# Gated attention and GEGLU on one core: row-tiled attention with turns of eight key tiles, one pool of eight PSUM banks, q, k, v and split weights by way of DRAM, and w_down's sums kept whole in PSUM

## Chip, cores and metric

The kernel runs on one core of a Trainium2 chip. The metric is the device time of one execution in microseconds, the median of several runs; smaller is better. PE is the matrix engine (TensorE), PEld its weight loads, DVE the vector engine, ACT the scalar engine, POOL GpSimd, SP the engine that sends most DMAs.

## What is computed

B = 1, S = 2048 tokens, D = 448, H = 16 heads of 28, F = 1792, all float32.

```python
def _A_ref(x, wqkv, wo):
    qkv = transpose((x @ wqkv).reshape(B, S, 3, H, Dh), 2, 0, 3, 1, 4)
    q, k, v = qkv[0], qkv[1], qkv[2]
    scores = einsum("bhqd,bhkd->bhqk", q, k) * (Dh ** -0.5)
    p = softmax(scores, axis=-1)
    return einsum("bhqk,bhkd->bhqd", p, v) ... .reshape(B, S, D) @ wo

def _B_ref(x, w_gate, w_up, w_down):
    return (gelu(x @ w_gate) * (x @ w_up)) @ w_down

g = sigmoid((x * gate_w).sum(-1, keepdims=True))
return g * _A_ref(x, wqkv, wo) + (1 - g) * _B_ref(x, w_gate, w_up, w_down)
```

## The kernel before

Nearly all matrix products are made in three passes: each float32 operand is split into a high part that TensorE multiplies fast (type fp32r) and a low part (operand minus high part); then high·high, low·high and high·low are summed. The split is a copy and a subtraction, on ACT, DVE or POOL.

The program has these stages. In the names, `hl` holds both parts of something, `u` is x·w_up, `gs` is x·w_gate, `pt` is a 128x512 tile of exponentials, `ps`, `sc`, `pv`, `pg` and `pd` are PSUM tiles (a bank each).

1. **QKV.** 28 tiles of q and k, transposed, 128 rows by 512 tokens (`pqk`, 308 matmuls), are split by ACT and DVE, and both parts are stored to DRAM (`qkd`, 28 stores of 512 KB). Then 16 tiles of V (`pv`, 176 matmuls); V stays in SBUF (`VA`). During the V tiles `X32`, x once more in a layout for row-tiled matmuls, is loaded and split (`split_x32`, L248 and L249). A bound of each head's scores is worked out for the softmax's shift and stored to `shd`; a branch that is not taken handles inputs for which that bound is too wide.
2. **Attention with the first feed-forward products.** A turn is one head and four key tiles (`TURN = 4`), 64 turns in all. TensorE's rows are used as four groups of 32: a matmul of a score (`sc<-Q,K`, contraction 28 rows and 2 shift rows) and one of x·w_up or x·w_gate (`ps<-X,w`, "cross") run beside each other, one in each row group. Four matmuls together are called a round here. After the rounds of a turn comes its values block (`ps<-pt,V`): four column groups, 32 matmuls in the trace. `plan()` simulates the engines with fixed costs and writes down the order of all of it, once, by hand; every instruction keeps that order on its engine. Four PSUM banks hold scores (`psc`), four the sums of cross products and values (`pss`); a cross group that a values block interrupts is added up in SBUF. Weight chunks of 21 cross products are loaded raw by SP in eight pieces (L262, buffer `wraw`) and split by DVE (L273, L275). Finished u and gs tiles go to DRAM (`ud`). ACT takes the exponential straight from the score's bank (L594), or DVE first copies the score to SBUF (L598). At the end of a head POOL's own DMA queue turns the denominators (`dend`, `r`, `rdend`, `rb`), POOL divides (L566) and stores the head's output (`od`).
3. **Transition.** The last gate block's products (`pg`, 168 matmuls) run after the last turn.
4. **Down.** For pairs of the 14 blocks of F (`FC = 2`) and four token blocks (`tb`): `hidden` loads u and gs, ACT applies gelu (L694), POOL multiplies (L695), ACT and DVE split (L696, L697); `down` sums two blocks in PSUM, and DVE adds each such sum into `acc` in SBUF (L714). `load_wo`, `load_o` and `project` bring wo and the attention's output in between.

The order in which DMAs leave SP is the program's. A DMA waits on SP for the one eight before it (they take eight semaphores in turn), and for the tile that it overwrites.

Of the kernel before, what the change touches and what calls it, by code (L numbers as in the profile page):

```python
# [17 lines left out]
P = 128  # L18
# [6 lines left out]
FC = 2  # L25
NB = NF - 1
ORDER = (NF - 1,) + tuple(range(NF - 1))
TURN = 4
LEAD = 8
FIRST = 16  # L30
RUN = 30
STEP, READ, SEEN = 227, 270, 200
EXP, EXP_OUT, COPY, BACK = 480, 620, 690, 100
VALUES, INTO, OUTOF = 857, 90, 200
AHEAD = 8
# [3 lines left out]
VP = H * VC + 8  # L39
# [4 lines left out]

PAIRS = [(b, w) for b in range(3) for w in (b, 4 + b)] + [(4 + b, b) for b in range(3)] + [(3, 3), (3, 7)]


def plan(count, parted=2, loaded=3):  # L50

    turns = [(h, kt) for h in range(H) for kt in range(0, NKT, TURN)]
    items = [[(i, (h, kt, qb)) for i, (h, k0) in enumerate(turns) for kt in range(k0, k0 + TURN)
              if kt // 2 % 2 == r % 2 for qb in (r // 2 * 2, r // 2 * 2 + 1)] for r in range(4)]
    total = count * 21
    ops = []
    now = act = dve = 0
    bank = [0] * 4
    score = [None] * 4
    pos = [0] * 4  # L60
    held = [False] * 4
    mine = [None] * 4
    free = [0] * 4
    shut = [False] * 4
    part = [False] * 4
    since = [0] * 4
    late = []
    left = [4 * TURN] * len(turns)
    seen = [0] * len(turns)
    turn_now = 0  # L70

    def run_act(i, key, src, ready):
        nonlocal act
        begin = max(act, ready)
        act = begin + EXP
        seen[i] = max(seen[i], begin + EXP_OUT + BACK)
        left[i] -= 1
        ops.append(("exp", key, src))
        return begin + EXP_OUT + BACK

    def run_late(until):
        late.sort(key=lambda a: (a[1], a[0]))
        while late and max(act, late[0][0]) <= until:
            ready, i, key = late.pop(0)
            run_act(i, key, None, ready)
# [6 lines left out]
    def end_score(r):  # L92
        i, key, b, _, keep = score[r]
        score[r] = None
        run_late(now + READ - 200)
        direct = max(act, now + READ) + EXP_OUT + BACK
        copied = max(dve, now + SEEN) + COPY + BACK
        if keep > 3 and copied - (200 if i > turn_now else 100) < direct and len(late) < 5:
            bank[b] = run_dve(now + SEEN)
            ops.append(("copy", key, b))  # L100
            late.append((bank[b], i, key))
        else:
            bank[b] = run_act(i, key, b, now + READ)

    def cross_ready(r):
        return (not shut[r] and pos[r] < total and (held[r] or free[r] <= now) and pos[r] // 21 < parted)

    def clear(r, ready):
        if held[r]:
            held[r] = False  # L110
            mine[r][4] = True
            free[r] = run_dve(ready)
            whole = pos[r] % 42 == 0
            ops.append(("clear", r, pos[r] - 1, part[r], whole))
            part[r] = not whole

    def step():
        nonlocal now
        did = []
        for r in range(4):  # L120
            if score[r]:
                i, key, b, n, _ = score[r]
                ops.append(("score", r, key, n, b))
                score[r][3] += 1
                did.append((r, True))
            elif cross_ready(r):
                ops.append(["cross", r, pos[r], not held[r], False])
                mine[r] = ops[-1]
                held[r] = True
                pos[r] += 1  # L130
                did.append((r, False))
        now += STEP
        for r, s in did:
            if s and score[r][3] == 3:
                end_score(r)
            if not s and pos[r] % 42 == 0:
                clear(r, now + SEEN)

    def run(number, n, count, first):
        nonlocal turn_now  # L140
        turn_now = number
        before, after = -(number - 1) % 4, -number % 4
        todo = [count] * 4
        done = k = 0
        n = max(n, first + 3 * count)
        while k < n or any(todo) or any(score):
            while done < 4 * count and k >= first and min(bank) <= now:
                can = [r for r in range(4) if todo[r] and not score[r]
                       and (r != after or todo[r] > 2 or k >= n - 6)]
                if not can or sum(map(bool, score)) >= 3:  # L150
                    break
                r = max(can, key=lambda r: (r == after and k >= n - 6, not cross_ready(r),
                                            not 0 < -pos[r] % 42 <= 2, todo[r], now - since[r]))
                since[r] = now
                b = bank.index(min(bank))
                bank[b] = 1 << 60
                score[r] = [*items[r].pop(0), b, 0, 4 * count - done]
                todo[r] -= 1
                done += 1
            if k >= n - 6 and not shut[after]:  # L160
                shut[after] = True
                clear(after, now + SEEN)
# [3 lines left out]
    def values(i):  # L166
        nonlocal now, parted, loaded
        h, k0 = turns[i]
        r = -i % 4
        while late and late[0][1] <= i:  # L170
            run_late(max(act, late[0][0]))
# [648 lines left out]
```

## Time and profile before

| | us |
|---|---|
| runs shown | 1095.02, 1092.5, 1093.34; median 1093.34 |
| profiled execution, device time | 1094.65 |
| its span | 1092.9 |
| mean clock of TensorE in it | 0.978 of full |
| qk tiles, until the first V tile | 77.8 |
| V tiles | 44.9 |
| attention, from its first matmul | 721.5 (123.36 to 844.89) |
| transition, until the first `pd` matmul | 36.4 |
| down and wo | 207.7 |
| tail | 4.0 |

How to read the rows that follow. In the page, the busy line gives busy time, share of the span and instructions of each engine. A window row gives start:end and length, then busy time and count of PE, PEld, DVE, ACT and POOL, then TensorE's granted clock (1.00 is full), the share of DMA engines in use and the GB/s that they moved. A group row gives line, engine, operation, output<-inputs, size and count, then busy time and mean ns of one, then the idle time of the engine ahead of them and what ended it. A timeline row gives the start, the length, engine and operation of a run of like instructions, and in brackets the idle time ahead and its releaser. A chain row gives a piece of the chain of work that ended last: start, length, what. A DMA row gives the queue, the count, the KB of one and the median us from issue to landing. Matmuls overlap, so that the mean duration of one (0.38 to 0.40 us) is longer than the step from one to the next.

### The profile page before, as it was taken

To read this page: it belongs to the slowest core of one execution; us is meant where nothing else is said; L and a number is where in the kernel's file an instruction comes from. 1 tells how busy PE (TensorE), PEld (TensorE's weight loads), DVE (VectorE), ACT (ScalarE), POOL (GpSimd) and SP (SyncE) were. 2 spreads that over 40 slices of the span, in tenths; PEclk is the share of its full clock that TensorE was granted. 3 is DMA by queue.
4 is the path that set the end of the run, shared out by engine and by line. 5 is a ranking of instruction groups with operands and counts; after the bars stand their busy time and mean duration, and the time that the engine had idled before them with its cause. 6 is when DMAs were issued, how large, how long until landed. Compare 5 with 4: busy or idle time off the path is not lost.

```text
span 1092.9 us, 28107 instructions
## 1 busy us (share of the span) xinstructions
PE 1024.8 (94%) x11191; PEld 741.9 (68%) x11191; DVE 692.5 (63%) x1121; ACT 654.2 (60%) x1255; POOL 271.4 (25%) x352
## 2 busy tenths in 40 slices
PE   9998599999999999999999999999999279889898
PEld 6887476666666666666767676766676267667787
DVE  5542266776666767586666776767765057777654
ACT  5333277777676767776767676767776044444330
POOL 5320100112122021221220212202212244444642
PEclk9999999999999999999999999999999779999999
DMA  8966244453443443534434444344423365665622
GB/s 268 339 231 155 72 128 123 121 165 114 122 149 104 144 135 110 152 109 142 156 95 141 120 144 150 105 139 127 140 82 92 112 223 174 210 185 185 203 91 101
DMA packets 102264, 160.00 MB, mean 146 GB/s; under 512 B 21360, under 2 KB 49776, under 8 KB 102128
## 3 DMA queue, kind: packets, MB, share of 16 engines
q1 hardware_dynamic: 92912, 144.90, 43.0%
q0 software_dynamic: 8384, 12.47, 4.1%
q8 instruction: 90, 1.47, 0.6%
q10 hardware_dynamic: 832, 0.79, 0.2%
q14 instruction: 46, 0.38, 0.1%
HBM read 107.21 MB, written 50.86 MB: 145 GB/s over the span
## 4 chain that ended last, share of the span: by engine, by line
PE 67%; issue 9%; POOL 6%; DMA 5%; DVE 1%; ACT 1%; SPq 0%; POOLq 0%; DVEq 0%; ACTq 0%
PE ps L205 45%; PE sc L205 20%; POOL g L695 4%; PE pd L205 2%; DMA oraw<-od 2%; DMA gs<-ud 1%; DVE hl L697 0%; ACT g L694 0%; POOL ohl L751 0%; SPq L262 0%; DMA u<-ud 0%; DVE ohl L750 0%; DMA draw<-in_wd 0%; DVE WO L737 0%; DMA dend<-o 0%
## 5 line engine op out<-in xcount | busy, mean ns | idle before, releaser
L205 PE MATMUL ps<-X,w 32*128 32x512 f32 x4536 | 480.9, 393 | 0.7 <-ACT gate L431 0.7
L594 ACT ACTIVATE pt<-sc 128x512 f32<-128x512 f32 x660 | 353.3, 608 | 194.8 <-PE sc L205 191.9
L205 PE MATMUL sc<-Q,K 32*128 32x512 f32 x3072 | 434.2, 404 | 9.0 <-DMA Q<-shd 9.0
L205 PEld LDWEIGHTS ps<-X,w 32*128 32x128 f32 x4536 | 387.1, 184 | 29.9 <-issue 10.1
L205 PEld LDWEIGHTS sc<-Q,K 32*128 32x128 f32 x3072 | 306.2, 183 | 76.1 <-issue 52.6
L598 DVE COPY pt<-sc 128x512 f32<-128x512 f32 x364 | 245.3, 689 | 62.9 <-PE sc L205 58.0
L205 PE MATMUL ps<-pt,V 128*32 128x512 f32 x2048 | 233.0, 595 | 0.1
L594 ACT ACTIVATE pt<-pt 128x512 f32<-128x512 f32 x364 | 221.5, 646 | 0.8 <-DVE pt L598 0.8
L205 PE MATMUL pd<-w,hl 128*128 128x448 f32 x672 | 150.2, 380 | 41.1 <-ACT hl L696 37.5
L205 PEld LDWEIGHTS pd<-w,hl 128*128 128x128 f32 x672 | 128.1, 193 | 62.6 <-ACT hl L696 40.2
L205 PEld LDWEIGHTS ps<-pt,V 128*32 128x32 f32 x2048 | 60.0, 109 | 138.0 <-issue 123.6
L635 DVE TENSOR_TENSOR o<-ps,o 128x512 f32<-128x512 f32 x48 | 33.2, 692 | 110.6 <-PE ps L205 110.6
L695 POOL TENSOR_TENSOR g<-g,u 128x512 f32<-128x512 f32 x56 | 73.3, 1314 | 87.7 <-ACT g L694 80.8
L551 POOL DMA_DIRECT2D dend<-o x64 | 31.7, 502 | 232.6 <-DVE o L635 166.6
L696 ACT ACTIVATE hl<-g 128x512 fp32r<-128x512 f32 x56 | 35.4, 632 | 80.1 <-POOL g L695 80.1
L613 DVE COPY u<-ps 128x512 f32<-128x512 f32 x108 | 72.1, 683 | 2.3 <-PE ps L205 1.3
L205 PE MATMUL pqk<-X,WQK 128*128 128x512 f32 x308 | 72.7, 397 | 0.4 <-ACT X L373 0.2
L275 DVE TENSOR_TENSOR w<-wraw,w 128x512 fp32r<-128x512 f32 x112 | 72.2, 684 | 0.0
L561 POOL DMA_DIRECT2D rdend<-r x16 | 8.9, 555 | 243.0 <-DVE r L560 243.0
L205 PEld LDWEIGHTS pqk<-X,WQK 128*128 128x128 f32 x308 | 57.7, 189 | 15.8 <-POOL WQK L383 1.3
L697 DVE TENSOR_TENSOR hl<-g,hl 128x512 fp32r<-128x512 f32 x56 | 43.6, 779 | 36.5 <-ACT hl L696 35.5
L714 DVE SCALAR_TENSOR_TENSOR acc<-pd,gate,acc 128x448 f32<-128x448 f32 x80 | 51.8, 676 | 8.7 <-PE pd L205 8.7
(78 smaller groups left out, 638.5 us busy)
## 6 DMA issues: line engine op xcount, KB each, us to landing
ud<-u SPq DMA_DIRECT2D x108, 256.0 KB
qkd<-hl SPq DMA_DIRECT2D x28, 512.0 KB
K<-qkd SPq DMA_DIRECT2D x128, 112.0 KB
Q<-qkd SPq DMA_DIRECT2D x128, 112.0 KB
u<-ud SPq DMA_DIRECT2D x56, 256.0 KB
gs<-ud SPq DMA_DIRECT2D x52, 256.0 KB
wraw<-in_wu SPq DMA_DIRECT2D x112, 64.0 KB
wraw<-in_wg SPq DMA_DIRECT2D x112, 64.0 KB
```

Source lines behind the costliest of these rows:

```text
L205: return pin(nc.tensor.matmul(o, lhsT, rhs, start=start, stop=stop))
L275: pin(nc.vector.tensor_tensor(w[:, 1, a], raw[:, a], w[:, 0, a].bitcast(F32), OP.subtract))
L551: pin(nc.gpsimd.dma_start(out=dend[h:h + 1, j * 512:(j + 1) * 512], in_=o[j * 32 + DH:j * 32 + DH + 1]))
L561: pin(nc.gpsimd.dma_start(out=rdend[h].rearrange("(p n) -> p n", p=P), in_=r))
L594: pin(nc.scalar.activation(PT[key], PT[key] if b is None else sc[b], AF.Exp, scale=SCALE))
L598: pin(nc.vector.tensor_copy(PT[key], sc[b]))
L613: pin(nc.vector.tensor_copy(u, ps[r]))
L635: pin(nc.vector.tensor_tensor(sums["o"], po, sums["o"], OP.add))
L695: nc.gpsimd.tensor_tensor(g, g, u, OP.mult)
L696: nc.scalar.activation(hl[:, 0], g, AF.Copy)
L697: nc.vector.tensor_tensor(hl[:, 1], g, hl[:, 0].bitcast(F32), OP.subtract)
L714: nc.vector.scalar_tensor_tensor(acc[:, t], p, g1, acc[:, t], OP.mult, OP.add)
```

## The change

- **Turns.** `TURN = 8`: 32 turns, each with a values block of eight key tiles. 36 tiles for exponentials are managed by `plan()`, as are the eight PSUM banks of one pool (`pk`): scores, cross sums and values take the bank that comes free first. Cross groups are shifted by `OFFSET` so that a group's sum stays in one bank; what the shift leaves over of the first block is done at the end and added (`again`).
- **q and k** are stored once as float32 (28 stores of 256 KB) and reloaded in pieces of 28x512 and 28x256, split by POOL; the shift rows go by POOL's queue, except for the first head.
- **V** is stored to DRAM by four DMAs of ACT's queue (5, 5, 3 and 3 tiles, runs of 580 and 348 bytes) and reloaded head by head (`VH`).
- **w_up and w_gate** are split once by POOL (`prepare`), stored split (`wsd`), and each chunk is loaded split, in eight DMAs of 32x2x512 or 32x2x384.
- **X32** is loaded and split by DVE among the qk tiles.
- **Down** runs token block by token block; the 14 blocks' sums stay in four PSUM banks, and DVE gathers once for each token block. Loads are issued four units ahead, and three units are loaded and multiplied ahead of `pg`. DVE multiplies (L726), ACT copies, DVE subtracts. POOL splits wo and the attention's output. The last head is divided after two units of the down stage.

The core of the diff:

```diff
-TURN = 4
-LEAD = 8
+TURN, LEAD, NPT, FIRST = 8, 4, 36, 16
+OFFSET = (0, 21, 9, 30)
...
-    qkd = dram.tile([2, 2 * D, S], F32, name="qkd")
+    qkd = dram.tile([2 * D, S], F32, name="qkd")
+    vd = dram.tile([P, H, NKT, VC], F32, name="vd")
+    wsd = dram.tile([2 * NF, P, 2, 4, P], F32, name="wsd")
...
+    def prepare(b):
+        raw = fw.tile([P, 4, P], F32, name="wraw", bufs=1)
+        by_sp(raw, src[f])
+        hl = fw.tile([P, 2, 4, P], F32R, name="whl", bufs=1)
+        parts(hl[:, 0], hl[:, 1], raw, pool_copy, pool_sub)
+        by_pool(wsd[b], hl.bitcast(F32))
+    def load_chunk(c):
...
-                pin(nc.sync.dma_start(out=raw[group(r), i:i + n], in_=src[f, 32 * j:32 * j + 32, 0:n]))
+                by_sp(w[group(r), :, i:i + n].bitcast(F32), wsd[b, 32 * j:32 * j + 32, :, 0:n])
...
+            if i == base + n - 1:
+                pin(nc.scalar.dma_start(out=vd[:, :, base:base + n], in_=V[:, :, 0:n]))
...
         def turn(i):
...
+            if h + 1 < H:
+                m0 = k0 // TURN * 2
+                if k0 == 0:
+                    for b in range(2):
+                        load_q(h + 1, b)
+                for m in (m0, m0 + 1):
+                    load_k(h + 1, m)
...
+        load_shift(0, by_sp)
+        load_v(0)
...
-            nc.gpsimd.tensor_tensor(g, g, u, OP.mult)
+        pin(nc.vector.tensor_tensor(u, g, u, OP.mult))
...
+    for n in range(1, 3):
+        multiply(n)
+        split_unit(n - 1)
+    PG = [bank(b) for b in early]
...
+    for n, (tb, f) in enumerate(UNITS):
...
+        if n + 4 < len(UNITS):
+            load_unit(n + 4)
+        if n + 3 < len(UNITS):
+            multiply(n + 3)
+        if n + 2 < len(UNITS):
+            split_unit(n + 2)
...
+        if n == 2:
+            divide()
+        if n == 3:
+            load_wo()
+        if n in (5, 10, 18, 32):
+            load_o((5, 10, 18, 32).index(n))
+        if f == 0 and tb:
+            project(tb)
+        down(n)
```

How it moves instructions, at three places. First SP's queue where the attention begins. `Q<-shd` are the shift rows of the first head, `wraw` raw weight pieces; the names in brackets are what a row waits for (DMAHW0 to DMAHW7 are the semaphores of DMAs, taken in turn). Before:

```order
L262 DMA wraw<-in_wu 32x384 [waits DMAHW3_49]
L262 DMA wraw<-in_wu 32x384 [waits DMAHW4_49]
L304 DMA Q_699<-shd 2x1024 [waits DMAHW5_49]
L304 DMA Q_699<-shd 2x1024 [waits DMAHW6_49]
L262 DMA wraw<-in_wu 32x512 [waits DMAHW3_49,DMAHW4_49,DMAHW1_49,DMAHW7_49,DMAHW0_49,DVE_49]
L262 DMA wraw<-in_wu 32x512 [waits DMAHW0_49]
L262 DMA wraw<-in_wu 32x512 [waits DMAHW1_49]
L262 DMA wraw<-in_wu 32x512 [waits DMAHW2_49]
```

And now, where `VH` is the first head's V, `qraw` the second head's raw q:

```order
L218 DMA Q_731<-shd 2x1024 [waits DMAHW4_49,DMAHW0_49]
L218 DMA Q_731<-shd 2x1024 [waits DMAHW5_49]
L218 DMA Q_731<-shd 2x1024 [waits DMAHW6_49]
L218 DMA Q_731<-shd 2x1024 [waits DMAHW7_49]
L218 DMA VH_5018<-vd 128x464 [waits DVE_49,DMAHW0_49,PE_49,Activation_49]
L218 DMA qraw_735<-qkd 28x512 [waits DMAHW1_49]
L218 DMA qraw_735<-qkd 28x512 [waits DMAHW2_49]
L218 DMA qraw_735<-qkd 28x512 [waits DMAHW3_49]
L218 DMA qraw_735<-qkd 28x512 [waits DMAHW4_49]
L218 DMA qraw_736<-qkd 28x512 [waits DMAHW5_49]
```

The weight chunk no longer stands among the four shift rows; instead VH, eight pieces of q and eight of k stand between them and the next chunk. DMAHW0 and DMAHW5 in the first two rows are the semaphores that the third and fourth store of V took on ACT's queue.

Second, TensorE at the start of the down stage (the numbers tell one tile from another). Before, with the two blocks of F in `hl2_17277` and `hl2_17290` and a bank `pd` for each of four token tiles:

```order
L205 MATMUL pd_17318<-w0_17267,hl2_17277 128x448 x3
L205 MATMUL pd_17318<-w1_17272,hl2_17290 128x448 x3
L205 MATMUL pd_17326<-w0_17267,hl2_17277 128x448 x3
L205 MATMUL pd_17326<-w1_17272,hl2_17290 128x448 x3
L205 MATMUL pd_17334<-w0_17267,hl2_17277 128x448 x3
L205 MATMUL pd_17334<-w1_17272,hl2_17290 128x448 x3
```

Now:

```order
L215 MATMUL b5_19496<-W0_19263,hl_19296 128x448 x3
L215 MATMUL b2_19497<-W0_19263,hl_19296 128x448 x3
L215 MATMUL b3_19498<-W0_19263,hl_19296 128x448 x3
L215 MATMUL b1_19499<-W0_19263,hl_19296 128x448 x3
L215 MATMUL b5_19496<-W1_19272,hl_19301 128x448 x3
L215 MATMUL b2_19497<-W1_19272,hl_19301 128x448 x3
```

A sum was complete after six matmuls; now four banks stay open, and each takes three matmuls of every block of F, 42 in all.

Third, DVE early in the down stage, before (`acc<-pd` takes a sum out of PSUM, `hl2` is the low part of a hidden tile):

```order
L697 TENSOR_TENSOR hl2_17277<-g_17280,hl2_17277 128x512
L697 TENSOR_TENSOR hl2_17290<-g_17293,hl2_17290 128x512
L712 TENSOR_SCALAR acc_17073<-pd_17318,gate_66 128x448
L697 TENSOR_TENSOR hl2_17300<-g_17303,hl2_17300 128x512
L712 TENSOR_SCALAR acc_17073<-pd_17326,gate_66 128x448
L697 TENSOR_TENSOR hl2_17308<-g_17311,hl2_17308 128x512
```

And now (`W` is w_down's low part, `hu<-hg,hu` the multiplication, `r` the last head's denominators):

```order
L225 TENSOR_TENSOR W4_19514<-draw_19512,W4_19514 128x448
L726 TENSOR_TENSOR hu_19487<-hg_19489,hu_19487 128x512
L225 TENSOR_TENSOR hl_19523<-hu_19288,hl_19523 128x512
L225 TENSOR_TENSOR W5_19540<-draw_19538,W5_19540 128x448
L726 TENSOR_TENSOR hu_19517<-hg_19519,hu_19517 128x512
L225 TENSOR_TENSOR hl_19549<-hu_19487,hl_19549 128x512
L571 RECIPROCAL r_19239<-r_19239 128x16
L225 TENSOR_TENSOR W6_19580<-draw_19578,W6_19580 128x448
```

For each block of F a subtraction of w_down, a multiplication and a subtraction of the hidden tile stand in a row, and no sum comes out among them; the sums follow after 14 blocks.

More of the change, by code (lines that the diff above doesn't have):

```diff
@@ L38 @@
 VC = DH + 1
-VP = H * VC + 8
 VW = 450
@@ L436, in gated_mix @@
             load()
-        for _ in range(4, AHEAD):
+        for _ in range(4, RAWS):
             load()
```

821 lines of the change are left out of this document (414 added, 407 removed).

## The prediction

> **What bounds the kernel now.** I read the page's shares and slices first, then the windows by stage, then the chain, and last the timeline around each gap. The page's busy line, and the windows (busy time and count of PE, PEld, DVE, ACT, POOL, then clock, DMA share, GB/s):
>
> ```profile
> PE 1024.8 (94%) x11191; PEld 741.9 (68%) x11191; DVE 692.5 (63%) x1121; ACT 654.2 (60%) x1255; POOL 271.4 (25%) x352
> GB/s 268 339 231 155 72 128 123 121 165 114 122 149 104 144 135 110 152 109 142 156 95 141 120 144 150 105 139 127 140 82 92 112 223 174 210 185 185 203 91 101
> 77.80:122.70 44.90, 38.52 (x205) 33.23 (x203) 13.79 (x24) 16.18 (x39) 2.28 (x2) 1.00 0.54 142
> 122.70:150.40 27.70, 18.06 (x244) 15.02 (x248) 10.32 (x17) 11.27 (x23) 1.81 (x1) 0.82 0.38 109
> 150.40:844.90 694.50, 694.44 (x9420) 462.76 (x9419) 482.43 (x812) 512.51 (x1006) 129.28 (x225) 1.00 0.43 127
> 844.90:881.30 36.40, 9.84 (x173) 8.66 (x169) 3.23 (x7) 5.24 (x8) 10.38 (x17) 0.69 0.43 131
> 881.30:1089.00 207.70, 188.00 (x848) 162.18 (x848) 140.91 (x198) 78.29 (x128) 94.73 (x75) 0.96 0.54 170
> 1089.00:1093.00 4.00, 0.00 (x0) 0.00 (x0) 0.68 (x1) 0.00 (x0) 0.00 (x0) 1.00 0.31 115
> ```
>
> TensorE bounds the attention completely: 694.44 of 694.50 us. It is not bound elsewhere: 6.4 us are idle in the V stage, 9.6 in turn 0 (first 27.7 us), 26.6 in the transition, 19.7 in the down stage. So the attention gets shorter only by fewer or better packed TensorE passes, and the other stages by fewer waits.
>
> The unit prices come from these rows of the timeline, the chain and the groups: the pg block (168 matmuls, 42 rounds of four row groups, nothing in its way), one values block with the round after it, the first and last values block of the 63 turns, the down and wo matmuls in a row.
>
> ```profile
> 844.89 9.84 PE L205 MATMUL pg<-X,w 32*128 32x512 f32 x168
> 447.85 3.64 PE L205 MATMUL ps<-pt,V 128*32 128x512 f32 x32
> 451.42 0.50 PE L205 MATMUL sc<-Q,K 32*128 32x512 f32 x3
> 150.40 3.57 PE ps L205 x32
> 841.39 3.67 PE ps L205 x32
> L205 PE MATMUL ps<-pt,V 128*32 128x512 f32 x2048 | 233.0, 595 | 0.1
> 1043.14 10.08 PE L205 MATMUL pd<-w,hl 128*128 128x448 f32 x48
> 1054.36 9.32 PE L205 MATMUL pd<-WO,ohl 128*128 128x448 f32 x44 [1.13 <-DVE y L717]
> ```
>
> A round: one matmul lasts about 0.39, so (9.84 − 0.39)/41 = 0.2305 us. A values block of four key tiles is 451.42 − 447.85 = 3.57 us, eight passes; its passes follow each other by (3.64 − 0.595)/7 = 0.435, so one more key tile (two passes) adds 0.87. A turn is (841.39 − 150.40)/63 = 10.97; without its values block 7.40, which for the 30.86 rounds of a turn (counted in program order: 2009 in all, 65 ahead of the first values block) is 7.11 + 0.29 of switching. Check: 2009 × 0.2305 + 64 × (3.57 + 0.29) = 710.1; the attention took 123.36 to 844.89 = 721.5, of which turn 0's waits explain 9.0 and a slow clock some 2. A down matmul is (10.08 − 0.38)/47 = 0.2065, a wo matmul (9.32 − 0.38)/43 = 0.208.
>
> **The change, part by part.**
>
> *Q, K, V.* The qk tiles are TensorE-bound and keep their 308 matmuls; the split of X moves among them and the subtraction of the qk eviction goes, so the V stage still starts at 77.8. There its only gap goes:
>
> ```profile
> L205 PE MATMUL pv<-WV,X 128*128 128x450 f32 x176 | 37.8, 370 | 6.3 <-ACT gate L431 6.3
> 123.36 3.94 PE L205 MATMUL ps<-X,w 32*128 32x512 f32 x64 [0.69 <-ACT gate L431]
> ```
>
> The gap is ACT, which waited in line 248 for raw X; no such split stands in the V stage now. V takes its busy 38.5 us; attention starts at 77.8 + 38.5 + 0.7 = 117.0 (before 123.4). If the new V stores or POOL's weight splits disturb it, all 6.4 come back.
>
> *Turns of eight, one bank pool.* 1955 rounds instead of 2009 (the floor, 7608 row-group matmuls over 4, is 1902). A values block has 3.57 + 4 × 0.87 = 7.05, plus 0.29, 32 times: 1955 × 0.2305 + 32 × 7.34 = 450.6 + 234.9 = 685.5 against 710.1. Of the 24.6 saved, 12.4 are rounds and 12.1 halved block starts. Cover for the other engines: copies to free banks rise from 364 to 452, but the weight splits leave DVE:
>
> ```profile
> L598 DVE COPY pt<-sc 128x512 f32<-128x512 f32 x364 | 245.3, 689 | 62.9 <-PE sc L205 58.0 <-ACT pt L594 0.8 <-PE ps L205 0.4
> L613 DVE COPY u<-ps 128x512 f32<-128x512 f32 x108 | 72.1, 683 | 2.3 <-PE ps L205 1.3
> L594 ACT ACTIVATE pt<-sc 128x512 f32<-128x512 f32 x660 | 353.3, 608 | 194.8 <-PE sc L205 191.9
> ```
>
> DVE: (452 + 111 + 32) × 0.69 = 411 of 690 us. ACT stays at 512 + a little of 685, three quarters. Neither bounds; for a values block that waits for a late exponential I add 2 us, between 0 and 0.29 again for each block (9).
>
> *The hand-over to attention.* Before, turn 0 stands still for Q's shift rows, which wait on SP behind a weight chunk:
>
> ```profile
> 130.31 0.87 PE L205 MATMUL sc<-Q,K 32*128 32x512 f32 x2 [3.01 <-DMA Q<-shd]
> 131.58 3.56 SPq L262 DMA_DIRECT2D wraw<-in_wu  x8
> 137.14 0.76 PE L205 MATMUL sc<-Q,K 32*128 32x512 f32 x1 [5.96 <-DMA Q<-shd]
> 135.19 1.81 DMA Q<-shd
> oraw<-od POOLq DMA_DIRECT2D x4, 768.0 KB, 6.8
> od<-o POOLq DMA_DIRECT2D x64, 56.0 KB, 2.2
> ```
>
> SP sends a DMA when the one eight before it has landed; eight of a chunk take 3.56, or 0.445 each. Afterwards the first shift rows, the first head's V (VH) and everything behind wait for the last store of V (712.7 KB, issued about 0.9 after V's last matmul). Its nearest row is 768 KB in 6.8, so it lands at +8; the second shift DMA 2 later, at +10, where group 2's first score (16 rounds in, +4.4) waits 5.6. Behind it VH, sixteen pieces of q and k and two stores go at 0.445, so chunk 3's fourth piece is sent at +18 and there at +20, while it is first used 10.6 us into attention, at +11.3: a stall of about 9 in all, no gain on the old 9. With a store that lands like 56 KB (2.2) it is 4; with one twice as slow, 16. I take 9, since 768 KB is nearly the size. The clock was 0.82 in the window of the old stall; (1 − 0.82) × 27.7 = 5 us of clock, part of them idle: 2 us lost, as in the check above, and again.
>
> The Trainium skill, page "DMA: Bandwidth & Descriptors", section Specifications, says that a transfer under 512 B is done as read-modify-write; the last two V stores write pieces of 348 B (the first two 580 B). No run so far shows such a store of this size; were it twice as long by that rule, the time would be some 7 us longer.
>
> *Reloaded chunks.* A weight chunk comes split, 917 KB instead of 459, in eight DMAs, and K and Q in smaller pieces: 959 SP DMAs in attention instead of 846. Sums of bytes: 82 MB become about 119 MB, 173 GB/s on average where a slice reached 339. From the order I counted the time between the last use of a buffer and the first use of its next chunk: at the prices above the shortest of 53 is 4.4 us, five are under 5.8, ten under 7, 18 under 8. Eight DMAs at 0.445 and a landing of 2.2 make 5.8: lateness 6 us, but each first matmul waits for its own group's piece alone, so 0 to 6; I take 1, inside the 2 above.
>
> *Transition.* The pg matmuls stay (9.84). Gone is the wait behind them:
>
> ```profile
> 862.84 1.84 DMA od<-o
> 864.82 3.47 DMA u<-ud
> 881.29 0.74 PE L205 MATMUL pd<-w,hl 128*128 128x448 f32 x1 [26.56 <-ACT hl L696]
> L695 POOL TENSOR_TENSOR g<-g,u 128x512 f32<-128x512 f32 x56 | 73.3, 1314 | 87.7 <-ACT g L694 80.8 <-DMA gs<-ud 5.1 <-DMA draw<-in_wd 1.3
> ```
>
> SP's first load of u waited for the last head's od, at 864.7. The new order loads and multiplies three units ahead of pg, and puts the division after two units. All 26.6 go if those loads land within attention and pg; cover 9.84 us against 2.2 to 6.8 for a load.
>
> *Down.* 672 × 0.2065 = 138.8 and 176 × 0.208 = 36.6: 175.4 instead of 207.7 (gone: 19.7 idle, the start at half clock, and the restarts). The multiply leaves POOL (1.31 us) for DVE, whose work per unit of 2.48 us of TensorE is multiply, subtraction and, in the first 14 units, the subtraction for w_down:
>
> ```profile
> L697 DVE TENSOR_TENSOR hl<-g,hl 128x512 fp32r<-128x512 f32 x56 | 43.6, 779 | 36.5 <-ACT hl L696 35.5
> L681 DVE TENSOR_TENSOR w<-draw,w 128x448 fp32r<-128x448 f32 x14 | 11.4, 817 | 25.0 <-ACT w L680 25.0
> L751 POOL TENSOR_TENSOR ohl<-oraw,ohl 128x1536 fp32r<-128x1536 f32 x4 | 14.0, 3502 | 4.0 <-ACT ohl L747 4.0
> L748 POOL CAST ohl<-oraw 64x512 fp32r<-64x512 f32 x4 | 2.4, 605 | 20.9 <-PE pd L205 17.7 <-DMA oraw<-od 3.2
> ```
>
> 0.78 + 0.78 + 0.82 + 0.2 for the sums = 2.58, 0.1 too much for 14 units: 1.4 us; afterwards 1.8 and hidden. POOL's chain to the first wo product: from unit 2 (+5) the division, 11.4 as it ran from 853.3 to 864.7, WO's cast and subtraction (1792 columns: 2.1 + 4.1), O's landing 6.8, its cast and subtraction 1.8 + 3.5 and small ones 1.2: 35.9 against 14 × 2.48 = 34.7. I take 3 us for both, between 0 and 20.
>
> *Sum:* 117.0 + 685.5 + 9.8 + 175.4 + 4.0 (last window) = 991.7 without a stall; + 9 + 2 + 2 + 3 = 1007.7. The profiled execution took 1094.65 for a span of 1092.9, so + 1.75; it lay 1.3 over the median, so − 1.3: **1008 us**.
>
> **Rivals.** *(b) The hand-over does not stall:* VH and chunk 3 come in time because the last V store lands in 2 to 3 us. 1008 − 11 = 997, or with the 5 us of small waits gone 992. Against it: the old queue stalled at exactly this place.
>
> *(c) Chunks late throughout:* if a piece lands after 5 us instead of 2.2 under the doubled traffic, a chunk needs 3.56 + 5 and 18 to 25 of 53 come late, 28 to 59 us by the sum of their lateness: 1036 to 1065. For it: 173 GB/s on average, large transfers at 6.6 to 6.8. Against it: half the peak slice, waits by group.
>
> *(d) The down stage is bound by loads or POOL:* the first 14 units need w_down, u and g of 0.75 MB in 2.48 us, 304 GB/s where the best slice was 339. At 200 GB/s they take 3.8 each: + 18, so 1026.
>
> *(e) Slower than before: SP's queue becomes the bound.* With eight in flight and in order, attention cannot be shorter than 959 × landing / 8. It decides from 690 us on, a mean landing of 5.8; the kernel gets slower than 1093.3 from (690 + 85) × 8 / 959 = 6.5 us; at the 6.8 of the large row it is 815, so 1008 + 125 = 1133. Against it: pieces of 28 to 131 KB are nearer to the 2.2 of 56 KB than to 768 KB.
>
> **How the numbers follow.** Forecast as summed 0.48 (its own range 998 to 1020); (b) 0.13; (d) 0.17; (c) 0.16; (e) 0.05; the rest 0.01 for no change. What can be told from no change is 0.2%, 2.2 us. All but (e) end faster: faster 0.94, same 0.01, slower 0.05. The range leaves out (e), the far third of (c) and the lower edge of (b): 989 to 1053.
>
> **What would show it.** V stage 38 to 39 us with PE busy throughout; attention start at 117; values blocks of about 7.05 and turns of 21.4; in turn 0 a TensorE gap of about 9 with the V store's landing ahead of it, released by Q<-shd and then the weight chunk; no gap after pg; units at 2.48. I am wrong if TensorE waits for w pieces beyond turn 0 (c), if its rounds are longer than 0.23 for lack of banks, or if the down stage waits on DVE's subtraction or the unit loads (d).

## The result: 4.0% faster, in the range but 41 us above the forecast

The changed kernel took 1049.08 us (median of 4 runs, 1047.02 to 1052.04), the kernel before 1093.12: ratio 0.9596, 95% interval 0.9568 to 0.9624. The forecast was 1008, its range 989 to 1053. The profiled execution took 1047.98 for a span of 1046.2; the forecast's span, worked out the same way, was 1007.7. Where the 38.5 us between the two lie is what the rest is about.

The page's busy line of the changed kernel, then windows by stage: V tiles, turn 0 up to its values block, the 31 turns to the last values block, that block, pg with the transition, and three pieces of the down stage (same columns as before):

```profile
PE 1001.7 (96%) x11191; PEld 762.1 (73%) x11191; DVE 559.1 (53%) x836; ACT 646.3 (62%) x1238; POOL 443.6 (42%) x646
77.80:116.86 39.06, 37.75 (x206) 33.68 (x205) 3.43 (x12) 9.88 (x32) 12.92 (x20) 1.00 0.80 185
116.86:162.20 45.34, 27.87 (x325) 22.17 (x325) 13.67 (x21) 15.36 (x31) 15.22 (x24) 0.74 0.60 169
162.20:831.30 669.10, 662.21 (x9271) 470.96 (x9267) 384.62 (x592) 513.83 (x989) 328.33 (x521) 1.00 0.60 181
839.20:853.07 13.87, 9.75 (x169) 9.10 (x169) 3.88 (x7) 4.85 (x8) 2.55 (x5) 0.93 0.89 286
853.07:889.00 35.93, 34.80 (x158) 31.32 (x159) 30.98 (x43) 23.00 (x44) 13.79 (x15) 0.93 0.89 302
889.00:925.00 36.00, 29.18 (x119) 24.89 (x118) 13.68 (x18) 4.09 (x7) 22.03 (x18) 0.86 0.53 168
925.00:1042.00 117.00, 116.45 (x573) 107.29 (x573) 68.20 (x94) 40.42 (x69) 16.88 (x12) 1.00 0.51 167
```

Of 45.34 us of turn 0 TensorE worked 27.87, at a mean clock of 0.74. The whole attention, 116.86 to 839.2, is as long as before (722 against 721.5): what turns of eight saved, their beginning and five late chunks ate. The gain comes from the stages around it: V 39 instead of 45, and 207 us from the end of attention to the end instead of 248.

Set against the forecast's sum, stage by stage (a priced row is the sum's own: rounds by 0.2305, blocks by 7.34, matmuls by 0.2065 and 0.208):

| stage | priced, no waits | forecast with waits | measured |
|---|---|---|---|
| start of attention | 117.0 | 117.0 | 116.86 |
| turn 0 (84 rounds, 116.86 to 162.23) | 19.4 | 30.4 | 45.4 |
| next 1871 rounds, 31 blocks (to 831.33) | 658.8 | 660.8 | 669.1 |
| last block and pg, to the first down matmul (853.07) | 17.2 | 17.2 | 21.7 |
| down, wo and tail, to the end | 179.4 | 182.4 | 193.1 |

So four terms were too small, by 15.0, 8.3, 4.5 and 10.7 us. TensorE's waits name them; the view gives us in total, times, longest:

```profile
PE b L215 <- DMA w<-wsd: 20.1, 10, 5.7
PE b L215 <- POOL ohl L225: 6.4, 4, 2.5
PE b L215 <- ACT hl L228: 4.1, 1, 4.1
PE b L215 <- DMA Q<-shd: 3.6, 1, 3.6
```

TensorE's timeline in turn 0, with the first values block, and SP's queue beside it:

```profile
119.93 1.09 PE L215 MATMUL b<-X,w 32*128 32x512 f32 x12 [1.91 <-DMA w<-wsd]
124.06 3.90 PE L215 MATMUL b<-X,w 32*128 32x512 f32 x36 [3.04 <-DMA w<-wsd]
130.93 2.04 PE L215 MATMUL b<-X,w 32*128 32x512 f32 x13 [2.97 <-DMA w<-wsd]
136.61 0.76 PE L215 MATMUL b<-Q,K 32*128 32x512 f32 x1 [3.63 <-DMA Q<-shd]
151.77 0.79 PE L215 MATMUL b<-X,w 32*128 32x512 f32 x2 [5.72 <-DMA w<-wsd]
162.23 7.07 PE L215 MATMUL b<-pt,VH 128*32 128x512 f32 x64
```

```profile
113.31 7.31 SPq L218 DMA_DIRECT2D w<-wsd  x6
120.73 4.81 SPq L218 DMA_DIRECT2D kraw<-qkd  x8
125.64 0.36 SPq L218 DMA_DIRECT2D wraw<-in_wu  x1
126.10 5.01 SPq L218 DMA_DIRECT2D w<-wsd  x8
134.78 1.16 SPq L218 DMA_DIRECT2D Q<-shd  x4
145.39 6.25 SPq L218 DMA_DIRECT2D w<-wsd  x8
SPq L218 <- DMA vd<-V: 15.7, 4, 7.1
```

The last row is SP's own waits from the V stage to 153 us. The forecast had SP send the first shift rows right when V ended and then stand still for the last V store. In fact SP was 18 us behind by then: it was still sending chunk 1 at 113 to 120, then pieces of k for the second half of the head, then chunk 2, and reached the shift rows at 134.78. It had waited 15.7 us for V's stores, four times: 10.7 by 114 us and 5.0 from 115.8 to 123.5. Another 3.7 us lie between the last piece of chunk 2 (sent by 131.11) and the first shift row: there stands the branch of L520, at which SP reads the flag and then waits for each of its eight DMA semaphores, so for what it has in flight. The forecast has no term for it.

### The profile page after: what moved, and what is told of

It is laid out like the page before. It is cut to its first block, busy times and chain, and to the rows that moved or that the text cites. A ratio compares the mean times of both kernels' runs of the same rounds, so it can differ in the third digit from the quotient of the medians.

```text
span 1046.2 us, 28127 instructions
## 1 busy us (share of the span) xinstructions
PE 1001.7 (96%) x11191; PEld 762.1 (73%) x11191; DVE 559.1 (53%) x836; ACT 646.3 (62%) x1238; POOL 443.6 (42%) x646
## 4 chain that ended last, share of the span: by engine, by line
PE 72%; DMA 7%; POOL 2%; SPq 2%; DVE 2%; issue 1%; ACT 1%; POOLq 0%; DVEq 0%; ACTq 0%
PE b L215 72%; DMA w<-wsd 3%; SPq L218 2%; DMA oraw<-od 1%; DMA hg<-ud 1%; DVE hu L726 1%; POOL ohl L225 1%; DMA rb<-rdend 1%; DMA draw<-in_wd 1%; DVE hl L225 1%; DMA rdend<-r 0%; POOL WO L225 0%; DVE y L750 0%; ACT hg L714 0%; POOL od L221 0%
## 5 line engine op out<-in xcount | busy, mean ns | idle before, releaser
L215 PE MATMUL b<-X,w 32*128 32x512 f32 x4704 | 479.5, 396 | 20.4 <-DMA w<-wsd 20.1
L215 PE MATMUL b<-Q,K 32*128 32x512 f32 x3072 | 448.9, 399 | 4.3 <-DMA Q<-shd 3.6
L215 PEld LDWEIGHTS b<-X,w 32*128 32x128 f32 x4704 | 416.1, 186 | 50.0 <-issue 25.5
L604 ACT ACTIVATE pt<-b 128x512 f32<-128x512 f32 x572 | 315.7, 604 | 184.7 <-PE b L215 157.9
L215 PEld LDWEIGHTS b<-Q,K 32*128 32x128 f32 x3072 | 358.4, 185 | 32.6 <-issue 17.0
L608 DVE COPY pt<-b 128x512 f32<-128x512 f32 x452 | 306.0, 690 | 86.8 <-PE b L215 64.3
L215 PE MATMUL b<-pt,VH 128*32 128x512 f32 x2048 | 227.5, 594 | 0.0
L215 PE MATMUL b<-W,hl 128*128 128x448 f32 x672 | 140.3, 370 | 5.8 <-ACT hl L228 4.1
L215 PEld LDWEIGHTS b<-W,hl 128*128 128x128 f32 x672 | 127.6, 190 | 18.0 <-ACT hl L228 4.5
L622 DVE COPY u<-b 128x512 f32<-128x512 f32 x108 | 73.0, 684 | 46.8 <-PE b L215 46.0
L224 POOL CAST whl<-wraw 128x512 fp32r<-128x512 f32 x28 | 17.2, 615 | 90.0 <-DMA wraw<-in_wu 50.4
```

Of the source, the lines that this page charges most:

```text
L215: return pin(nc.tensor.matmul(o, lhsT, rhs, start=start, stop=stop))
L224: pin(copy(hi, src))
L604: pin(nc.scalar.activation(PT[key], PT[key] if b is None else sc[b], AF.Exp, scale=SCALE))
L608: pin(nc.vector.tensor_copy(PT[key], sc[b]))
L622: pin(nc.vector.tensor_copy(u, ps[b]))
```

## Experiments

All ratios are to the kernel before on the same chip; the changed kernel's is 0.9596. Stage lengths are read from each kernel's timeline as in the table above.

**Turn 0: is it the stores' small pieces?** V is stored as four sets with one contiguous run for each partition.

```diff
-    vd = dram.tile([P, H, NKT, VC], F32, name="vd")
+    vd = dram.tile([4, P, H, 4, VC], F32, name="vd")
...
-                pin(nc.scalar.dma_start(out=vd[:, :, base:base + n], in_=V[:, :, 0:n]))
+                pin(nc.scalar.dma_start(out=vd[base // 4], in_=V))
```

> The changed kernel with V kept in DRAM as four sets of four tiles, each stored as one contiguous run of 7424 bytes per partition instead of pieces of 580 and 348 bytes; the reload of a head takes pieces of 464 bytes. Theory 1 (the V stores' small pieces hold the DMA engines and, through the semaphores that SP's DMAs share with them, SP's queue: 15.7 us of SP's waits in the V stage): SP's wait on the stores falls under 6 us, TensorE's waits in turn 0 from 17.5 to under 6, the first values block starts some 15 us earlier, device time 1028 to 1036. Rival (SP simply has too many bytes to send ahead of the first shift rows: 0.6 us for each DMA): turn 0 gains under 4 us, time 1045 or more.

Measured: 1044.61 us, ratio 0.953 (0.9496 to 0.9564). Turn 0 took 44.0 instead of 45.4, a gain under 4 as the rival had it; V is 1.1 shorter and the later turns 3.1, and what follows them is 2.1 longer. The small pieces alone are not it; SP still waits for the stores, and the shift rows still leave at 134:

```profile
102.88 12.86 SPq L218 DMA_DIRECT2D w<-wsd  x8
134.08 1.16 SPq L218 DMA_DIRECT2D Q<-shd  x4
SPq L218 <- DMA vd<-V: 12.4, 4, 5.7
```

Eight pieces of chunk 1 took 12.86 us here: the third store was only sent at 107.06, when ACT had come to V tile 11. Theory 1 as stated fell. (Of the time from chunk 2 to the shift rows 6.0 us are the branch here.)

**The same pieces by POOL's queue.**

```diff
-                pin(nc.scalar.dma_start(out=vd[:, :, base:base + n], in_=V[:, :, 0:n]))
+                by_pool(vd[:, :, base:base + n], V[:, :, 0:n])
```

> The changed kernel with the four V stores, same pieces, sent by POOL's queue instead of ACT's, so that SP's DMAs share no semaphore with them. Theory 1a (it is the shared semaphores): SP's wait on the stores goes, turn 0's waits fall from 17.5 to under 6, time about 1030. Theory 1b (it is the DMA engines that the small pieces fill: busy share 1.15 to 1.25 in the records): SP's DMAs land late anyway, turn 0's waits stay over 12, time 1043 to 1050. If POOL's splits of k are delayed by the stores, it can be up to 10 us slower.

Measured: 1061.54, ratio 0.9693 (0.9665 to 0.9721), slower. Half of theory 1a came out: the shift rows left at 121.78 instead of 134.78, and turn 0 took 33.6 instead of 45.4. But the V stage itself broke. POOL, which works in order, had splits of k ahead of the second store and stood 15.3 us idle for that k, so the second store left only at 119.6, and V's two buffers came free late:

```profile
121.78 3.34 SPq L218 DMA_DIRECT2D Q<-shd  x4
109.99 9.52 PE L215 MATMUL pv<-WV,X 128*128 128x450 f32 x33 [3.78 <-ACT gate L228]
131.48 4.49 PE L215 MATMUL pv<-WV,X 128*128 128x450 f32 x11 [11.97 <-ACT gate L228]
```

**Only the place in the program.** Chunks 1 and 2, k's second half and the third block's split are moved ahead of V tile 4; in the second run the second head's q and k go behind chunk 3 as well.

```diff
+        load_chunk(1)
+        for m in range(2, 4):
+            load_k(0, m)
+            split_k(0, m)
+        prepare(2)
+        load_chunk(2)
         for i in range(4, NT):
             last = v_tile(i)
-            if i == 5:
...
```

> The changed kernel with chunk 1, the rest of the first head's k, the third block's split and chunk 2 moved ahead of V tile 4 in the program, and so ahead of the first V store. Theory 1c (not how long a store takes, but its place: an SP DMA that shares its semaphore with a store waits until ACT has come to that V tile and the store has landed): SP's waits on the stores before the branch go, the first shift rows are sent by 125 instead of 134.8, TensorE's waits in turn 0 fall from 17.5 to 8 to 11, and the first values block starts 8 to 14 us earlier; time 1034 to 1041. Rival (SP's queue has too many bytes ahead of the shift rows): shift rows not before 132, gain under 3 us, time 1046 or more.

> As the run before it, and the second head's q and k are loaded behind chunk 3 instead of ahead of it. If chunk 3 is late because VH and sixteen pieces of q and k stand ahead of it, its wait (5.7 us) goes as well: 4 to 7 us under the run before it, time 1029 to 1036. Rival (chunk 3 is late because its buffer comes free late): no difference from the run before it.

Measured: 1050.97, ratio 0.9582 (0.9561 to 0.9603), and 1047.36, ratio 0.9556 (0.9513 to 0.9599). The rows are the first run's. Theory 1c fell in this form: SP waited longer for V's stores, not less (17.3 us): the semaphores still go round through ACT's stores, and already chunk 0's second piece waits 6.8 for the first of them (7.1 in the changed kernel). The shift rows left at 138.50. The second run shortened turn 0 by 5.6 (39.9 against 45.5 in the first), as expected, but its chunks 2 and 3 stay late, and 4.5 of the 5.6 are lost again in the later turns (674.1 against 669.6). Nor is 5.6 much: in the profiled executions of four kernels that are alike up to the end of turn 0 (the changed one and, below, those for the gap ahead of the down stage and for the wo products) it took 45.4, 48.4, 50.7 and 45.9. The two ratios do not tell the two runs apart.

```profile
106.46 17.21 SPq L218 DMA_DIRECT2D w<-wsd  x8
138.50 1.22 SPq L218 DMA_DIRECT2D Q<-shd  x4
SPq L218 <- DMA vd<-V: 17.3, 4, 6.8
```

**Both together: another queue, and nothing ahead that isn't needed.** V's stores by POOL; VH, k's second half, the third block's split and the second head's q and k behind chunk 3.

```diff
+                by_pool(vd[:, :, base:base + n], V[:, :, 0:n])
...
         def load(c):
             load_chunk(c)
+            if c == 3:
+                load_v(0)
+                for m in range(2, 4):
+                    load_k(0, m)
+                    split_k(0, m)
+                prepare(2)
+                turn_loads(0)
```

> The changed kernel with the V stores on POOL's queue, and the loads of the first head's second half of k, of the third weight block and of VH and the second head moved behind chunk 3 in turn 0, since none of them is used before the first values block. Theory 1d (turn 0 is lost because SP's one queue, eight in flight, carries V's stores in its rotation and loads that nobody needs yet ahead of the first shift rows and chunks 1 to 3): SP waits for no V store in the V stage, the shift rows are sent by 119, TensorE's waits in turn 0 fall from 17.5 to under 6 with less slow clock, the first values block comes some 22 us after the attention's start instead of 45; time 1024 to 1032. Rival (the DMA engines are full at that place, in whatever order): turn 0 still over 35 us, time over 1040.

Measured: 1045.57, ratio 0.9546 (0.9517 to 0.9574). SP no longer waits for a V store in the V stage, TensorE's waits in turn 0 fall from 17.5 to 5.3, and none is for a weight piece; turn 0 takes 30.9 instead of 45.4. But 6.0 of that are lost again in V, where ACT stands 7.5 us for a buffer of V whose store has not landed; POOL's stores land late (rows of the DMA view: KB, median us to landing). And the shift rows leave at 128, not by 119: SP's sixteen pieces of chunks 1 and 2 take until 121.72, and then it stands 6.4 us at the branch, most of it waiting for what it has in flight (second row, of SP's waits):

```profile
111.74 10.83 PE L215 MATMUL pv<-WV,X 128*128 128x450 f32 x44 [4.29 <-ACT gate L228]
SPq L515 <- SPq L515: 4.8, 5, 3.6
128.16 1.18 SPq L218 DMA_DIRECT2D Q<-shd  x4
vd<-V POOLq DMA_DIRECT2D x2, 1160.0 KB, 12.7
vd<-V POOLq DMA_DIRECT2D x2, 696.0 KB, 8.5
```

The first values block stands 8.5 us earlier (153.72 against 162.23); 3.4 of these are lost in later turns and 2.6 in the down stage, which the edit does not touch.

**Late chunks after turn 0.** Each of the late chunks stands in SP's queue right behind a store of u that waits for DVE's copy. One of them: TensorE's wait, SP's rows, and SP's waits from 336 to 349:

```profile
348.19 0.47 PE L215 MATMUL b<-X,w 32*128 32x512 f32 x1 [2.31 <-DMA w<-wsd]
342.11 0.34 SPq L218 DMA_DIRECT2D ud<-u  x1
342.56 5.95 SPq L218 DMA_DIRECT2D w<-wsd  x8
SPq L218 <- DVE u L622: 3.9, 1, 3.9
```

So each store was sent one tile later:

```diff
-            by_sp(ud[n // 42 % (len(BLOCKS) - 1), :, r * TB:(r + 1) * TB], u)
+            while hold:
+                by_sp(*hold.pop(0))
+            hold.append((ud[n // 42 % (len(BLOCKS) - 1), :, r * TB:(r + 1) * TB], u))
```

> The changed kernel with each store of a u tile sent one tile later on SP, so that no chunk load stands behind a store that waits for DVE's copy. Theory 2 (the five late chunks after turn 0 stand behind such a store, which waited 3.9 to 5.2 us for DVE): TensorE's 6.3 us of waits on weight pieces after turn 0 go, with the slow clock behind the longest of them; the 31 turns after the first values block take 661 instead of 669, time about 1041. Rival (a chunk's eight pieces take 6 us by themselves and come late anyway): under 3 us gained, time 1046 or more.

Measured: 1045.62, ratio 0.9547 (0.9525 to 0.9569). The turns from the first to the last values block take 660.62 instead of 669.1, with TensorE busy 659.72, and 0.4 us of waits on weight pieces are left there of 6.3. Theory 2 holds, with its size, in the profiled execution; that one is the fastest of the four (1040.95), and the median is only 3.5 under the changed kernel, where 8 were expected. What the other executions lost was not profiled.

```profile
163.42:824.04 660.62, 659.72 (x9269) 469.71 (x9267) 384.04 (x592) 513.56 (x989) 327.01 (x521) 1.00 0.63 183
```

**The gap ahead of the down stage.** The chain of the changed kernel there:

```profile
843.45 5.58 DMA draw<-in_wd
849.11 0.58 ACT W L228
849.70 1.28 ACT L714
851.00 0.64 ACT hg L714
853.44 0.61 ACT hl L228
```

```diff
-    for n in range(4):
-        if n < 3:
-            load_f(n)
-        load_unit(n)
+    load_unit(0)
+    load_unit(1)
     multiply(0)
+    load_f(0)
...
```

> The changed kernel with the first hidden tiles loaded and multiplied ahead of w_down's first three blocks, on SP and on ACT. Theory 3 (the 4.1 us gap ahead of the down stage is the queue order: the chain goes from the third w_down load over ACT's split of it and then gelu): the gap falls to under 1.5 us, the slow clock behind it (6.8 us at half) goes too, time 1041 to 1045. Rival (loads only start when attention has ended, land after 5.6 us, and the chain behind them is as long): gap 3 us or more, time 1046 or more.

Measured: 1053.32, ratio 0.9615 (0.9597 to 0.9633). The gap fell from 4.1 to 2.4, between the two theories, and the time did not fall; turn 0 was 3.0 longer in the profiled execution, which the edit does not touch. Unclear: what gain there is lies below what these runs tell.

**The wo products' waits on POOL.** First the chain starts earlier, then its result is used later.

```diff
-        if n == 2:
-            divide()
-        if n == 3:
-            load_wo()
+        if n == 0:
+            divide()
+            load_wo()
```

> The changed kernel with the last head's division and wo's load and split at the first unit of the down stage instead of the third and fourth. Theory 4 (the waits of the wo products, 6.8 us on POOL's splits and some 5 us of slow clock behind them, come from a POOL chain that starts at 860.6, where DVE's reciprocal stands behind two units, and is 36 us long): the chain starts some 5 us earlier, the waits on POOL fall under 2 us, time 1038 to 1042. Rival (the chain is paced by its DMAs and POOL's splits of O for the second block, not by its start): waits stay over 4 us, time 1045 or more.

Measured: 1052.9, ratio 0.9602 (0.9581 to 0.9624): no gain (the profiled execution has a turn 0 of 50.7, which the edit does not touch, and a down stage of 194.5 against 193.1). The chain's start moved from 21.5 us after attention to 18.2, but its end only from 58.6 to 57.8, and 6.8 us of waits stayed, as the rival had it. In the changed kernel the chain is paced by landings: the row of O in the chain takes 7.54, and POOL idles 5.39 for the reciprocals:

```profile
873.40 1.29 POOL L576 TENSOR_TENSOR o<-o,rb 128x512 f32<-128x512 f32 x1 [5.39 <-DMA rb<-rdend]
884.49 7.54 DMA oraw<-od
```

```diff
-        if f == 0 and tb:
+        if f == 0 and tb > 1:
             project(tb)
+        if n in (17, 24):
+            project((17, 24).index(n))
...
-            if tb == 0:
-                project(tb)
```

> The changed kernel with the first two wo products after units 17 and 24 instead of 13 and 14. Theory 4b (POOL's chain to O ends 58.6 us after attention; it is paced by its DMAs under the down stage's loads, so only a later use hides it): the 6.8 us of waits on POOL go, with the slow clock at 895 to 902 and 912 to 916; time 1038 to 1042. Rival (the down stage is slow from the loads' bandwidth, not from this wait): under 4 us gained.

Measured: 1040.32, ratio 0.9495 (0.947 to 0.952). No wait on POOL is left, the slow clock behind it is gone, and the stage to the end takes 184.7 instead of 193.1. Theory 4b holds. The gap ahead of the stage grew meanwhile, from 4.1 to 7.3: the third load of w_down took 8.0 instead of 5.6 to land. The edit does not touch that load, and why it took longer is open. The two rows are the down stage of this kernel and of the changed one:

```profile
854.03:1038.70 184.67, 177.67 (x848) 160.28 (x848) 114.21 (x154) 67.39 (x120) 52.59 (x44) 0.99 0.61 199
853.07:1046.20 193.13, 180.82 (x848) 163.52 (x848) 113.98 (x154) 67.51 (x120) 52.70 (x44) 0.96 0.59 193
```

**What turns of eight are worth.** The changed kernel with turns of four; with the same offsets the leftover of the first block is done before the point at which the kernel fetches what it must be added to, so that this addition is left out (a copy of the same size stands in its place).

```diff
-TURN, LEAD, NPT, FIRST = 8, 4, 36, 16
+TURN, LEAD, NPT, FIRST = 4, 4, 36, 16
...
```

> The changed kernel with turns of four key tiles: 64 turns, 2008 rounds instead of 1955 by the same planner, 64 values blocks of 3.57 instead of 32 of 7.05. By the prices of the sum (0.2305 for a round, 3.86 and 7.34 for a block) the attention gets 12.2 + 12.1 = 24 us longer, time 1073. Rival (rounds were not the bound, the blocks' starts are hidden): under 10 us longer. Second rival (a turn of four leaves the exponentials less time ahead of their block): over 35 us longer.

Measured: 1086.16, ratio 0.9934 (0.9908 to 0.996), 37 us above the changed kernel: with turns of four and everything else changed, nearly the whole gain over the kernel before is gone. The price from rows accounts for 24. From the start of the first values block to that of the last (871.51) the 63 turns take 715.6, where 1951 rounds and 63 blocks of 3.86 make 692.9; 6.4 of the 22.7 between are waits that TensorE's timeline shows (2.2 of them for exponentials, the second rival). Of the other 16.3 half is a miscount. 2008 counts rounds in program order. In the last turns, where the products with x have run out, the planner takes scores two at a time, a step for row groups 0 and 1 and one for 2 and 3; such a pair was counted as one round, 34 times, so the planner's steps are 2042. In the eight turns with four such pairs a turn lasts 1.14 us more than its price and waits, in the 54 with none 0.14: the pairs cost two rounds, 34 × 0.2305 = 7.8 in all, and the price becomes 32. That leaves some 8 us, or 0.13 for each block, without a named wait: open. Turn 0 lost nearly the same as with turns of eight, 23.4 against 26.0 (36.5 for 57 rounds, 13.1), so its loss has little to do with the turn's length.

**The losses together.** V's stores on POOL with the loads behind chunk 3, stores of u one tile later, wo later.

> The three changes together: V stores on POOL with the loads behind chunk 3, the stores of u one tile later, the first wo products later. If the three losses are separate, their gains add: some 21 + 8 + 9 us from 1049, 1008 to 1016, which is the forecast's own sum. If they trade the same time, over 1022.

Measured: 1024.54, ratio 0.9355 (0.9327 to 0.9382): the fastest version here, 2.5% under the changed kernel. The parts add up but for the hand-over, which yields 7.5 instead of 21: V 6.6 longer, turn 0 31.3 instead of 45.4 (SP stands 7.2 at the branch, and the shift rows leave at 129), the turns 662.9, the down stage and tail 180.1, 0.7 over the price without waits. Against the waitless sum of 991.7 (span 1022.6) 30.9 are left: 6.5 in V, 11.9 in turn 0, 4.1 in the turns, 7.7 ahead of the down stage, 0.7 in it.

```profile
123.47:154.75 31.28, 25.96 (x325) 21.09 (x326) 13.90 (x21) 15.83 (x31) 8.43 (x13) 0.84 0.53 139
842.52:1022.60 180.08, 174.96 (x848) 160.84 (x848) 117.18 (x154) 67.48 (x120) 53.32 (x44) 0.98 0.61 204
```

**A third V buffer.** As that, with V in sets of three tiles through three buffers, so six stores, and the first hidden tiles ahead.

```diff
-        VSETS = {0: (VS[0], 5), 5: (VS[1], 5), 10: (VS[0], 3), 13: (VS[1], 3)}
+        VSETS = {3 * j: (VS[j % 3], 3 if j < 5 else 1) for j in range(6)}
```

> As the kernel with the three changes together, and V goes to DRAM in sets of three tiles by way of three buffers (six stores), and the first hidden tiles are loaded ahead of w_down's. If the 6 us that the V stage lost when its stores went to POOL are a wait for one of two buffers, the attention starts at 117 to 118 again, and the gap ahead of the down stage shrinks by some 2 us: 1013 to 1019. If the V stage's stall is POOL's in-order queue itself, no gain: 1022 to 1027.

Measured: 1042.34, ratio 0.9507 (0.9486 to 0.9529), 18 us slower than without. Attention started at 123.97 instead of 123.47, and turn 0 took 41.4. ACT still stands 8.0 us for a store of V (6.9 in the run before), so neither theory's time came. Every store has 2048 pieces (348 bytes, in the last one 116); their median landings, SP's sixteen weight pieces beside them, and one window:

```profile
vd<-V POOLq DMA_DIRECT2D x5, 696.0 KB, 18.1
vd<-V POOLq DMA_DIRECT2D x1, 232.0 KB, 17.5
99.05 33.50 SPq L218 DMA_DIRECT2D w<-wsd  x16
104.00:112.00 8.00, 6.83 (x34) 5.94 (x32) 0.00 (x0) 1.22 (x4) 1.11 (x1) 1.00 1.04 135
```

The medians are not the price of a single store. The first store, with no other in flight, landed 6.8 us after it was sent; the other four of 696 KB took 16.6 to 22.0, each sent before the one ahead had landed; and the 232 KB landed 1.9 us after the store ahead of them. In the window the DMA engines' packets fill a share of 1.04 at 135 GB/s, where the changed kernel moved 302 in the down stage with a share of 0.89. SP's sixteen pieces of weights took 33.5 us meanwhile, 22.6 in the run before. So at this place six stores hold up everything else. That the size of their pieces does it is likely but not shown: this run has more stores as well as smaller pieces. Contiguous stores (the first experiment) on POOL's queue were not tried together; whether they bring turn 0 to its price is open.

## Why the forecast was right, and where it was wrong

- *That 1049 lies in the range is in part luck.* The sum's own range ended at 1020. What reaches from there to 1053 is there for rivals (d), 1026, and (c), 1036 and more. The mechanism of (c) did not come and that of (d) only in part; four losses, all on one side, took their place. Of the 85 us forecast 44 came.
- *The unit prices held.* pg took 9.86 (9.84 before), a values block 7.07 (forecast 7.05), attention started at 116.86 (117.0), and with the late chunks gone the 31 turns took 660.6 (658.8). With 1.1 us of waits left, the down stage and tail took 180.1 (179.4).
- *The hand-over was mis-sized: 26.0 instead of 11* (turn 0 45.4, its rounds 19.4). The step that failed is "afterwards the first shift rows ... wait for the last store of V". The place and the queue were right; the length was not, because only the last store was counted. All four stores sit in the rotation of eight semaphores, so SP lost 10.7 us among the V tiles already and 5.0 around their end; what the V stage sends behind them (k's second half, a third block) was taken as out of the way; and the branch, 3.7 us, was not counted. Taking the first two away together turns 17.5 us of waits into 5.3; what each is worth alone, these runs do not separate. In place of the 2 us of slow clock stand some 8.5 (26.0 less the 17.5 of waits).
- *The last store's length.* The last store, 696 KB in pieces of 348 bytes, was sent at 117.18 and had its last packet at 122.8, 5.6 us later; the first, 1160 KB in pieces of 580, took 7.8. So the last one was not twice as long as the forecast's 6.8. In the packets' records the median is 0.021 us for 348 bytes and 0.034 for 580, the same for each byte; the means, 0.035 and 0.041, are worse for the small ones. The Trainium skill, page "DMA: Bandwidth & Descriptors", section Specifications, has a read-modify-write below 512 B; no doubling is seen in these records, and whether the worse mean is that or the load of the moment stays open.
- *Chunks: "lateness 0 to 6; I take 1" was 6.3,* plus 1.7 of slow clock and 0.6 of another wait. The count of buffer times left out that SP sends in order, and that a u store waiting for DVE stands ahead of the chunk. The term of 3.56 for a chunk's eight pieces was small too: the split pieces take SP 5.01 even where none waits (the row at 126.10). Rival (c), taken as 28 to 59 us, did not come: at 181 GB/s and a DMA share of 0.60 only five chunks were late, each behind such a store.
- *Transition: 4.1 of 26.6 stayed.* The cover of "9.84 us against 2.2 to 6.8 for a load" was right for the loads (5.58), but SP sends them only after the last chunk (839.6), and behind the landing stand w_down's split, 1.28 on ACT ahead of gelu, gelu, the product and the split.
- *Down: "3, between 0 and 20" was 13.7.* DVE's own work was not the cause: subtraction of w_down 0.63, product and split 0.68 each, 2.0 for a unit instead of 2.58. But it grows while POOL computes. 98 of the 112 products and splits have no POOL computation beside them and take 0.67 to 0.69; of the 14 beside one, 13 take 1.1 to 4.5. This one ran beside POOL's subtraction for WO (878.82 to 883.21), and TensorE's wait of 1.1 on DVE follows at its end:

```profile
879.22 4.54 DVE L225 TENSOR_TENSOR hl<-hu,hl 128x512 fp32r<-128x512 f32 x1
```

The larger loss was POOL's chain: it ended 58.6 us after attention where the forecast's durations make 50.7 (9.8 of pg, 5 and 35.9), and made 6.8 us of waits; 1.7 are waits on DVE, and some 5 slow clock. That is rival (d)'s place, at less than its price.
- *Rival (e), SP's queue as the bound,* did not come: SP sent 978 DMAs in those 722 us, and TensorE waits 6.3 us for weight pieces after turn 0.

## What to carry to other kernels

A DMA that one engine issues can stand in the way of another engine's queue when the two take semaphores from one rotation; so ask of each new store not only how long it takes, but when its engine will get to send it, and which loads come eight places behind it. Sum a queue from where it really stands at the hand-over, not from an empty start, and move behind the first need whatever is not needed before it. A result that comes late off a side engine is cheaper to use later than to make earlier, when its chain is paced by landings.

## What was unexpected of the hardware

Stores on one queue held each other up: the first store of 696 KB in 2048 pieces landed 6.8 us after it was sent, the next four 16.6 to 22.0 us, while the DMA engines' packets filled a share of 1.0 with 129 to 135 GB/s. In that run, from 85 to 160 us, the packets of these stores (mostly 4176 bytes, twelve pieces of 348) took 0.45 us on average, those of two stores of split weights (4096 bytes in one piece) 0.17, one of the two at a quieter time.

DVE's products and splits of a hidden tile took 0.68 us each, and 1.1 to 4.5 us beside a computation of POOL in 13 of 14 cases.

From the start of attention on, each of the changed kernel's pauses of TensorE from 1.9 us up (1.91 to 5.72) has a stretch of 3.4 to 10.2 us at half the clock at it or behind it in the trace's clock records; those of 1.8 us and less started none. So a wait cost about half as much again: 26.0 us lost for 17.5 of waits in turn 0, at a mean clock of 0.74.
